# Dense matmuls beside P*V bursts issued as four 32-column tiles, with new orders on all five engines

## The chip, the core and the metric

The kernel runs on one core of one Trainium2 chip. The metric is the time of one execution on the device in microseconds (us). TensorE (PE in the profile; its weight loads are listed as PEld) does the matrix products, VectorE (DVE), ScalarE (ACT) and GpSimd (POOL) the elementwise work, and SyncE (SP) issues most of the transfers (DMAs) between device memory and the core. ScalarE's queue issues the transfers of wk and wv.

## What is computed

A sequence of 2048 tokens of width 512 goes through two branches, and a sigmoid gate for each token mixes the two results. Branch A is an attention with 32 heads of width 16, in four segments of 512 tokens: causal softmax attention inside a segment, and beside it a linear memory that carries the segments before. Branch B is a gated feed-forward layer of width 1792.

```
g = sigmoid((x * gate_w).sum(-1))
for s in range(4):                       # branch A, 512 tokens at a time
    p = softmax(qs @ ks.T * 0.25 + mask);  a_dot = p @ vs
    a_mem = (phi(qs) @ M) / (phi(qs) @ z + 1e-6)
    o = sig(beta) * a_mem + (1 - sig(beta)) * a_dot
    M, z = M + phi(ks).T @ vs, z + phi(ks).sum(0)
a = concat(o) @ wo
b = (gelu(x @ w_gate) * (x @ w_up)) @ w_down
out = g * a + (1 - g) * b
```

## The kernel before

The work is cut into named tasks of a few instructions. For a segment s, `K`, `Q` and `V` are the projections, `G` and `U` the gate and up products of branch B, and `D` the down product together with the product by wo. All of these are dense: 128 rows by 128 weight columns, 512 values long (256 long in `K0`; 384 and 128 long in the last tile of the output). They are made by `mm` (L502) and cut by `pieces` (L506) into tasks of mostly two matmuls, such as `G1_7.0` and `G1_7.2`. Each task name in an order list stands for such a piece.

The attention of a segment has four steps t. A step has four score visits `qkS_tA0`, `B0`, `A1`, `B1`, and in the even steps a fifth, `L`. A score visit is a set of matmuls of 32 rows by 128 columns (L872): four heads at a time, each in its own 32 rows of the array. ScalarE then takes the exponential of all four PSUM banks (L878), GpSimd masks it (L881), and two tasks `pvS_t_j` on TensorE multiply by V (L920, L928). Those are column tiles: 128 rows by 17 weight columns, four heads beside each other at columns 0, 32, 64 and 96. The memory update `mzS` (L839) has the same form with 32 weight columns. So TensorE works in three forms, and passes from one to another at each change of kind: 32-row tiles (scores, and the memory's read `numx` at L792), full 128x128 (dense), and 32-column tiles (P*V and memory update).

PSUM has eight banks. Four belong to the scores and four, `psW0` to `psW3`, go round between all other products.

The order of the work is written out by hand: `ORDER` (L41) has one list of task names for each engine. `schedule` (L238) does not choose an order. It walks the lists, gives PSUM banks to the tasks, and keeps a clock of its own with costs such as `SWITCH` (L32) for a change of form on TensorE and `BLOCK`, `BLOCK_ASK`, `BLOCK_END` (L35) for the fetches of TensorE's instructions. For the first transfers, that clock has fixed times by name, in the table `LANDING` (L37):

```
            if t.name in LANDING:
                avail = max(t.finish + 2.3, LANDING[t.name])
```

Those times do not depend on where a transfer's name stands in its list. The instructions of each engine are then emitted in the order of its list, with semaphore waits for what they read and overwrite.

The start matters for what follows. Eight matmuls on constants, `warm0` to `warm7` (L590), need no data. Then 16 transposes `x0t...` (L599) turn the first segment's x, which arrives in two transfers `x0_0` and `x0_1` into hT (L574, 256 KB each, 1 KB being 1024 bytes). ScalarE and VectorE copy the result to xT, and the 32 pieces of `K0` follow. A piece whose number after the point is 0 or 2 needs the first part of wk (`w_wk0`, 128 KB); the others need `w_wk1` (128 KB) or `w_wk2` (256 KB). Q0 needs `w_wq0` and `w_wq1`, V0 needs `w_wv0` and `w_wv1` (256 KB each), G0 and G1 need `w_wg0` and `w_wg1` (896 KB each). SyncE issues x, wq and wg; ScalarE issues wk and wv.

The names at the end: `D3_3` is the last tile of the output, in two parts of 384 and 128 columns; ScalarE scales and stores the first (L1048) and VectorE the second (L1051).

Of the kernel before, what the change touches and what calls it, by code (L numbers as in the profile page):

```python
# [21 lines left out]
P = 128  # L22
# [12 lines left out]
BLOCK, BLOCK_ASK, BLOCK_END = 254.4, 172, 192  # L35
# [52 lines left out]
    "act": (  # L88
# [14 lines left out]
    "dve": (  # L103
# [37 lines left out]
class Instr:  # L141
    __slots__ = ("fn", "reads", "writes", "est", "dma_sem", "waits", "deps", "inc", "fence")

    def __init__(self, fn, reads=(), writes=(), est=0.1, dma_sem=None):
# [8 lines left out]
        self.waits = []  # L153
        self.deps = []
        self.inc = False
        self.fence = False


class Grp:
# [268 lines left out]
def _build(es, nc, A_x, A_wq, A_wk, A_wv, A_wo, A_beta, B_w_gate, B_w_up, B_w_down, gate_w, out):  # L428
# [33 lines left out]
    gmat = gexp  # L462
# [707 lines left out]
```

## Time and profile before

| | |
|---|---|
| median of 3 runs | 265.47 us (265.13 to 265.95) |
| the profiled execution | 265.32 us |
| its span in the profile | 264.1 us |
| TensorE matmuls, busy | 3153, 261.1 us (99%) |
| ScalarE busy | 209.0 us (79%) |
| VectorE busy | 197.5 us (75%) |
| GpSimd busy | 105.7 us (40%) |
| instruction fetches (DMA queue q8) | 25 packets, 0.41 MB |

The 1.2 us between the span and the execution's time lie around the profiled instructions. A busy TensorE in this profile only means that matmuls are in flight; their ends are modelled and overlap. So it is read by the starts: the difference between the starts of two groups in the timeline is what the first group cost.

### The profile page before, as it was taken

Reading aid. Unit: us, or ns where it says so; the run is one execution under the profiler, and the core shown is the slowest. Engines: PE = TensorE matmul, PEld = TensorE weight load, DVE = VectorE, ACT = ScalarE, POOL = GpSimd, SP = SyncE. Lnnn points to the kernel's source line nnn. Section 1 sums busy time; section 2 is a strip of 40 time slices with the busy share of each in tenths; the row PEclk is TensorE's granted clock in tenths of the full one; section 3 lists DMA queues with packets and bytes.
Section 4 is the critical chain, followed back from the end, with each engine's and each line's share of the span. In section 5 each row is a group of like instructions: output and inputs, shape, how many; then the busy total and the mean of one; then the engine's idle time right before and its main releaser. Section 6 shows DMA issues by size and latency. Waiting matters only on the chain.

```text
span 264.1 us, 7382 instructions
## 1 busy us (share of the span) xinstructions
PE 261.1 (99%) x3153; PEld 117.6 (45%) x3153; DVE 197.5 (75%) x376; ACT 209.0 (79%) x179; POOL 105.7 (40%) x256
## 2 busy tenths in 40 slices
PE   8999999999999999999999999999999999999997
PEld 4644444444444434443544434353444433443453
DVE  0778788999997968889897776779887751485671
ACT  3698988998999788798877887788787787776702
POOL 8206686352600067265300274608470108352510
PEclk9999999999999999999999999999999999999999
DMA  6962117900003894420004251200000021401002
GB/s 224 320 175 49 37 24 196 243 4 0 2 10 112 224 178 81 64 82 0 2 0 67 57 132 32 83 2 20 5 2 0 2 63 31 91 2 42 22 0 82
DMA packets 32769, 18.25 MB, mean 69 GB/s; under 512 B 20576, under 2 KB 32736, under 8 KB 32736
## 3 DMA queue, kind: packets, MB, share of 16 engines
q1 hardware_dynamic: 31632, 16.73, 26.3%
q10 hardware_dynamic: 1104, 1.05, 1.2%
q8 instruction: 25, 0.41, 0.7%
q14 instruction: 8, 0.07, 0.1%
HBM read 9.84 MB, written 2.10 MB: 45 GB/s over the span
## 4 chain that ended last, share of the span: by engine, by line
PE 96%; DMA 1%; ACT 1%; DVE 0%; issue 0%; ACTq 0%
PE psW L503 75%; PE psXALL L872 9%; PE psW L920 6%; PE psXALL L503 3%; PE psW L928 1%; DMA hT<-in_A_x_dram 1%; PE psW L839 1%; ACT pt L878 1%; PE psXALL L792 1%; PE psXALL L599 1%; ACT L878 0%; DVE obf L1051 0%; ACTq L399 0%
## 5 line engine op out<-in xcount | busy, mean ns | idle before, releaser
L878 ACT ACTIVATE pt<-psXALL 128x2048 bf16<-128x2048 f32 x64 | 120.1, 1876 | 27.1 <-PE psXALL L872 23.5
L881 POOL TENSOR_SCALAR_AFFINE_SELECT pt<-pt 128x256 bf16<-128x256 bf16 x128 | 58.8, 471 | 103.0 <-ACT pt L878 98.2
L503 PE MATMUL psW<-xT,wu 128*128 128x512 bf16 x224 | 55.2, 380 | 0.0
L503 PE MATMUL psW<-xT,wg 128*128 128x512 bf16 x224 | 54.2, 380 | 0.0
L503 PE MATMUL psW<-wd,hT 128*128 128x512 bf16 x210 | 54.1, 380 | 0.0
L1019 DVE TENSOR_TENSOR hT<-psW,hT 128x512 bf16<-128x512 f32 x56 | 36.8, 683 | 16.5 <-PE psW L503 16.2
L881 POOL TENSOR_SCALAR_AFFINE_SELECT ptl<-ptl 128x512 bf16<-128x512 bf16 x32 | 22.5, 702 | 38.0 <-ACT ptl L878 36.4
L503 PEld LDWEIGHTS psW<-xT,wu 128*128 128x128 bf16 x224 | 20.3, 98 | 25.7 <-issue 2.7
L503 PEld LDWEIGHTS psW<-xT,wg 128*128 128x128 bf16 x224 | 20.6, 98 | 24.7 <-issue 2.1
L934 DVE STREAM_TRANSPOSE tb<-psW 128x512 f32<-128x512 f32 x32 | 21.5, 699 | 11.7 <-PE psW L928 11.5
L503 PEld LDWEIGHTS psW<-wd,hT 128*128 128x128 bf16 x210 | 19.3, 98 | 23.9 <-issue 3.0
L872 PE MATMUL psXALL<-qT,kpad 32*128 32x320 bf16 (+3 forms) x512 | 25.4, 273 | 0.0
L1003 ACT ACTIVATE hT<-psW 128x512 bf16<-128x512 f32 x28 | 15.7, 596 | 5.5 <-PE psW L503 5.4
L503 PE MATMUL psW<-xT,wk 128*128 128x512 bf16 (+1 forms) x80 | 19.0, 343 | 0.0
L920 PE MATMUL psW<-pt,vaug 128*17 128x192 bf16 (+3 forms) x512 | 18.8, 273 | 0.0
L872 PEld LDWEIGHTS psXALL<-qT,kpad 32*128 32x128 bf16 x512 | 7.6, 92 | 24.5 <-ACT pt L878 15.4
L503 PE MATMUL psW<-wv,xT 128*128 128x512 bf16 x64 | 18.5, 380 | 0.0
L878 ACT ACTIVATE ptl<-psXALL 128x2048 bf16<-128x2048 f32 x8 | 15.0, 1876 | 3.8 <-PE psXALL L872 3.6
L503 PE MATMUL psW<-wo,oT 128*128 128x512 bf16 x60 | 16.8, 380 | 0.0
L1068 DVE TENSOR_SCALAR ost<-psW,omgt 128x512 bf16<-128x512 f32 x9 | 6.7, 746 | 11.9 <-PE psW L503 11.9
L520 DVE CAST hT<-psW 128x512 bf16<-128x512 f32 x19 | 12.8, 684 | 3.7 <-PE psW L503 3.5
L779 POOL COPY exsT<-exs 32x4 f32<-32x4 f32 x64 | 13.9, 217 | 3.7
(104 smaller groups left out, 302.2 us busy)
## 6 DMA issues: line engine op xcount, KB each, us to landing
out_dram<-ost SPq DMA_DIRECT2D x15, 128.0 KB, 1.9
wg<-in_B_w_gate_dram SPq DMA_DIRECT2D x2, 896.0 KB, 7.3
wu<-in_B_w_up_dram SPq DMA_DIRECT2D x2, 896.0 KB, 6.8
wd<-in_B_w_down_dram SPq DMA_DIRECT2D x2, 896.0 KB, 7.2
phkt<-in_A_x_dram SPq DMA_DIRECT2D x3, 512.0 KB, 4.6
vlow<-vaug SPq DMA_DIRECT2D x8, 136.0 KB, 2.8
hT<-in_A_x_dram SPq DMA_DIRECT2D x2, 256.0 KB, 3.9
wq<-in_A_wq_dram SPq DMA_DIRECT2D x2, 256.0 KB, 5.3
```

The costliest lines, as they stand in the source:

```text
L503: return Instr(lambda e: e.matmul(view(), lhsT, rhs, start=first, stop=last), reads=reads, writes=[fkey if fkey is not None else g.key], e ...
L520: alts[DVE] = [Instr(lambda e: e.tensor_copy(dst(), src()), reads=reads, writes=writes, est=dve_t(n))]
L599: task(f"x0t{nm}_{u}", PE, [Instr(lambda e, k=k, a=a, u=u, k0=k0, src=src: e.transpose(src[:, k, a * 128:(a + 1) * 128], xin[:, 2 * u + a, ...
L779: cross = task(f"exsT{s}", POOL, [Instr(lambda e, g=g, c=c: e.tensor_copy(exsT[sl][32 * g:32 * g + 32, c:16:4], exs[32 * c:32 * c + 32, s4 ...
L872: instrs.append(Instr(lambda e, g=g, lhs=lhs, rhs=rhs, c0=c0, ncol=ncol: e.matmul(X[g][:, c0:c0 + ncol], lhs(32 * g), rhs(32 * g), start=T ...
L878: exp_task(s, f"exp{s}_{t}{name}", [Instr(lambda e: e.activation(dst[:], XALL[:, :].rearrange("p (g c) -> p g c", g=4), ACTF.Exp, scale=AT ...
L881: task(f"msk{s}_{t}{name}", POOL, [Instr(lambda e, view=view, pat=pat, base=base: e.affine_select(out=view, in_=view, compare_op=ALU.is_ge ...
L920: instrs.append(Instr(lambda e, t=t, q=q, kb=kb, slot=slot, c0=c0: e.matmul(gp.f32()[32 * q:32 * q + 17, 128 * kb + 64:512], Vaug[sl][:, k ...
L934: task(f"pvt{s}_{t}_{j}", DVE, [Instr(lambda e: e.transpose(Tb[:, j, :], gp.f32()[:, :]), [gp.key], [("Tb", j)], dve_t(512))], grp=gp)
L1003: lambda e, g=g, ft=ft, s=s: e.activation(hT[s % 2][:, ft, :], g.f32()[:, :], ACTF.Gelu_apprx_tanh),
L1019: task(f"Um{s}_{ft}", DVE, [Instr(lambda e, g=g, ft=ft: e.tensor_tensor(hT[sl][:, ft, :], g.f32()[:, :], hT[sl][:, ft, :], ALU.mult), [g.k ...
L1068: DVE: [Instr(lambda e, view=view, gt=gt, tile=tile: e.tensor_scalar(ostage[(4 * s + tile) % N_OST][:], view(), omgt[:, gt:gt + 1], None, ...
```

## The change

A new method `column_runs` looks at TensorE's list. It cuts the list at every task of the 32-row form (`qk` and `numx`). In a stretch between two cuts that holds at least one `pv` or `mz` task, all pieces made only by `mm` are marked. A marked matmul is emitted as four matmuls of 32 weight columns each, at column positions 0, 32, 64 and 96. All four read the same 512 moving values, and write their 32 partitions of the same PSUM bank. Only the last of the four signals.

```
+    def column_runs(tasks):
+        run = []
+        for t in tasks + [None]:
+            if t is not None and t.tiled != "qk":
+                run.append(t)
+                continue
+            if any(u.tiled == "pv" for u in run):
+                for u in run:
+                    if all(i.wide for i in u.alts[PE]):
+                        u.tiled = "pv"
+                        for i in u.alts[PE]:
+                            i.cols = True
+            run = []
...
-                n_ins = 2 * len(t.alts[PE])
+                n_ins = sum(8 if i.cols else 2 for i in t.alts[PE])
...
     def mm(g, view, lhsT, rhs, reads, first, last, n, fkey=None):
-        return Instr(lambda e: e.matmul(view(), lhsT, rhs, start=first, stop=last),
-                     reads=reads, writes=[fkey if fkey is not None else g.key], est=mm_t(n))
+        def f(e):
+            if not ins.cols:
+                return e.matmul(view(), lhsT, rhs, start=first, stop=last)
+            for c in range(0, P, 32):
+                r = e.matmul(view()[c:c + 32, :], lhsT[:, c:c + 32], rhs, start=first, stop=last,
+                             tile_position=(0, c))
+            return r
+        ins = Instr(f, reads=reads, writes=[fkey if fkey is not None else g.key], est=mm_t(n))
+        ins.wide = True
+        return ins
```

`BLOCK_ASK` and `BLOCK_END` go from 172 and 192 to 187 and 207. All five lists of `ORDER` are new; the tasks in them are the same 615 on TensorE. The parts of the lists that the prediction speaks of:

```
 sp, head
-  x0_0 x0_1 w_wq0 w_wq1 w_wg0 x1_0 w_gwb x1_1 w_beta x1_2 x1_3 w_wg1
+  w_wg0 x0_0 x0_1 w_wq1 w_beta x1_1 w_wq0 x1_0 x1_2 w_wg1 w_gwb x1_3
 act, head
-  tload w_wk0 w_wk1 w_wk2 w_wv0 x0ev0b_0 w_wv1 x0ev1_0 K0_1ev
+  w_wk2 w_wk1 w_wv0 w_wk0 tload x0ev0b_0 w_wv1 x0ev1_0 x0ev1_1
 pe, after the eight warm tasks
-  x0t0a_0 x0t0b_0 x0t1_0 K0_0.0 K0_2.0 K0_3.0 x0t0_1 K0_3.1
+  x0t0a_0 x0t1_0 x0t0b_0 K0_3.0 K0_1.0 K0_0.0 K0_2.0 x0t0_1
 pe, one stretch with P*V
-  qk1_0B0 pv0_3_1 pv0_3_0 U1_8.0 U1_11.2 U1_8.2 U1_6.0 qk1_0L
+  qk1_0B0 U1_0.2 pv0_3_1 U1_13.2 U1_9.0 U1_10.0 U1_9.2 pv0_3_0 qk1_0L
 pe, end
-  D3_2.14 D3_2.16 D3_3w0.12 D3_3a0.0 D3_3w1.4 D3_3w1.8 D3_3w1.12 D3_3a1.0
+  D3_2.16 D3_3w0.12 D3_1.16 D3_3a1.0 D3_0.16 D3_3a0.0
```

In the new list of TensorE 22 stretches hold a P*V or memory task. 218 dense matmuls stand in them and become 872.

More of the change, by code (lines that the diff above doesn't have):

```diff
@@ L34 @@
 TABLE = 1.3
-BLOCK, BLOCK_ASK, BLOCK_END = 254.4, 172, 192
+BLOCK, BLOCK_ASK, BLOCK_END = 254.4, 187, 207
 DMA_SPARE = 1.6
@@ L42 @@
     "pe": (
[45 rows of a table removed]
-    "act": (
[14 rows of a table removed]
-    "dve": (
[18 rows of a table removed]
-    "pool": (
[13 rows of a table removed]
[44 rows of a table added]
+    ),
+    "act": (
[15 rows of a table added]
+    ),
+    "dve": (
[17 rows of a table added]
+    ),
+    "pool": (
[7 rows of a table added]
+    ),
[6 rows of a table added]
+    ),
 }
@@ L141 @@
 class Instr:
-    __slots__ = ("fn", "reads", "writes", "est", "dma_sem", "waits", "deps", "inc", "fence")
+    __slots__ = ("fn", "reads", "writes", "est", "dma_sem", "waits", "deps", "inc", "fence", "wide", "cols")
     def __init__(self, fn, reads=(), writes=(), est=0.1, dma_sem=None):
@@ L156, in __init__ @@
         self.fence = False
+        self.wide = self.cols = False
 class Grp:
@@ L236, in add @@
         return task
+    @staticmethod
+    def column_runs(tasks):
[11 more added lines that the diff above has]
+            run = []
     def schedule(self):
@@ L240, in schedule @@
         queue = {e: [named[x] for x in reversed(ORDER[e].split())] for e in ENGINES}
+        self.column_runs([named[x] for x in ORDER[PE].split()])
         n = len(named)
```

177 rows, old and new, of the table ORDER are left out of this document.

## The prediction

> **What bounds the kernel now.** I read the page first, then the waits of TensorE, then its starts in the timeline, and for the head the transfers.
>
> ```profile
> PE 96%; DMA 1%; ACT 1%; DVE 0%; issue 0%; ACTq 0%
> ```
> ```profile
> PE psW L590 <- PEq L1155: 0.8, 1, 0.8
> PE psXALL L599 <- DMA hT<-in_A_x_dram: 0.2, 1, 0.2
> ```
>
> The chain that ended last is TensorE almost all the way, and the waits of TensorE are two: the start of the program, and 0.2 us at 4.36 us, for the first half of x. After that, it always has a matmul ready. So whatever makes its list shorter makes the kernel shorter, and whatever holds it up is lost for good. What the list costs is read from the starts (timeline of TensorE, 38 to 45 us; first column the start, xN the instructions):
>
> ```profile
> 38.26 0.81 PE L839 MATMUL psW<-vaug,phkt 128*32 128x34 bf16 x64
> 39.00 0.60 PE L503 MATMUL psW<-xT,wg 128*128 128x512 bf16 x2
> 39.54 0.40 PE L872 MATMUL psXALL<-qT,kpad 32*128 32x448 bf16 x8
> 39.87 0.60 PE L503 MATMUL psW<-xT,wg 128*128 128x512 bf16 x2
> 40.31 0.59 PE L503 MATMUL psW<-wv,xT 128*128 128x512 bf16 x2
> 40.74 0.59 PE L503 MATMUL psW<-xT,wk 128*128 128x512 bf16 x2
> 43.34 1.03 PE L503 MATMUL psW<-xT,wg 128*128 128x512 bf16 x4
> 44.29 0.62 PE L920 MATMUL psW<-pt,vaug 128*17 128x448 bf16 x16
> 44.73 0.29 PE L928 MATMUL psW<-ptl,vlow 128*17 128x64 bf16 x16
> ```
>
> Two dense matmuls inside a dense stretch take 40.74 - 40.31 = 0.43, 0.216 each. Two with a change of form behind them take 39.54 - 39.00 = 0.54, four take 44.29 - 43.34 = 0.95 instead of 0.86. So a change costs about 0.096. The single starts of the trace give medians of 88 to 97 ns over what the columns need, whichever two forms are changed, and 10 ns more on the second matmul after each entry into the dense form.
>
> **Part 1: fewer changes of form.** Counted along TensorE's list, there are 170 changes before: 64 dense to score, 68 score to dense, 7 score to P*V, 11 P*V to score, 12 dense to P*V, 8 P*V to dense. After, the marked pieces have the form of the P*V bursts: 54, 53, 22 and 21, and none of the last two kinds, 150 in all. 20 x 0.096 = 1.92, and 23 fewer entries into the dense form at 0.010 = 0.23. **-2.15 us**, all on TensorE's path.
>
> **Part 2: a dense matmul as four column tiles.** Not in the trace of before, but its P*V bursts have that form. Sixteen of them, 448 + 320 + 192 + 64 = 1024 columns in each of the four tiles, take 44.73 - 44.29 = 0.44. Two dense matmuls, also 1024 columns, take 0.43. So the four tiles do run side by side, at 0 to 5 ns more for 512 columns; for 218 matmuls that is 0 to +1.1. I take 0: 0.43 and 0.44 differ by a last digit. Weight loads: 64 memory matmuls, each with its own load of 32 columns, take 39.00 - 38.26 = 0.74, less one change 0.64, so 10 ns for load and matmul. A group's four need 40 ns and lie under its 216, also under the 55 ns of the 18 short groups (128 columns) of the last tile. The Trainium skill, "TensorEngine Tiling (Array Packing)", Restrictions and Gotchas, says that column tiling excludes the fast weight load; with the load time of "TensorE: Matmul & The Clock Gate", LDWEIGHTS, (columns over 1.2 per ns) four loads would take 107 ns, and as an estimate the 18 short groups would cost 0.9 us more. The row of 10 ns speaks against it, and the sum goes by the row.
>
> **Part 3: instructions.** 218 x 3 more matmuls and as many loads are 1308 instructions. The page has 6306 of TensorE in 25 fetch packets, 252 each: 5 fetches more. A packet takes 0.7% of 16 engines' span / 25 = 1.2 us. Where marked pieces and bursts stand thickest (the last 15 us) a packet's worth lasts about 5 us by the durations above, so its successor has time to come. Cost 0; if that cover were gone, up to 5 x 1.2 = 6.
>
> **Part 4: the end.** Now the 384-column part is last (`D3_3a0.0`). Its copy on ScalarE takes 0.58, VectorE's of 128 columns took 0.35, and its last matmul is longer: **+0.3**. In the body, the new lists move nine tasks from VectorE to ScalarE, about 0.6 each; at 79% and 75% busy both stay beside TensorE, cost 0.
>
> **Part 5: the head of the transfer queues.** This decides. SyncE's list now begins with `w_wg0`, 896 KB, ahead of x; ScalarE's puts the first part of wk last of four. Issue times on SyncE, and what the transfer page says of two of them (the first x, then wg; last number: us from issue to landing):
>
> ```profile
> 0.81 0.96 SPq L534 DMA_DIRECT2D hT<-in_A_x_dram  x2
> 2.83 0.47 SPq L534 DMA_DIRECT2D wg<-in_B_w_gate_dram  x1
> ```
> ```profile
> hT<-in_A_x_dram SPq DMA_DIRECT2D x1, 256.0 KB, 3.5
> ```
> ```profile
> wg<-in_B_w_gate_dram SPq DMA_DIRECT2D x1, 896.0 KB, 9.1
> ```
>
> x landed at 4.31, wg, issued at 2.83, at 11.9. SyncE's queue (q1) serves in order: in the packet records wg's packets of 1792 bytes begin at 7.4, when the 1024 KB of x and wq ahead of it have gone. How fast bytes move, in two stretches (last number GB/s):
>
> ```profile
> 0.00:4.36 4.36, 3.36 (x9) 1.03 (x9) 0.00 (x0) 1.49 (x2) 3.21 (x14) 1.00 0.48 154
> 4.36:8.20 3.84, 3.84 (x37) 3.42 (x38) 1.14 (x3) 1.25 (x3) 3.67 (x3) 1.00 1.10 358
> ```
>
> 671 KB (of 1000 bytes) by 4.36, then 358 a microsecond, with engines full. Ahead of the end of both `x0_0` and `w_wk0` now stand 896 + 256 KB on SyncE's queue and 768 KB on ScalarE's, 1966 of 1000 bytes. (1966 - 671) / 358 = 3.62: done at 8.0. If the queues take turns by packet (1792 against 1024 bytes for wg, then equal), each gets there at 8.0. Landing follows the last byte by 0.63 (3.68 to 4.31 before). x at 8.6 against 4.31, so the transposes start **4.25 us later**, and K0, 0.8 behind, too. Ends: if SyncE's queue gets ahead (70 of 100 packets), x comes at 7.4, but wk only at 10.05, against K0's start at 5.18: +4.9. The least is wk at 8.4, x earlier: +3.25. Nothing hides it: TensorE has no idle time later to give back.
>
> It is also cold. The timeline from 0.84 us:
>
> ```profile
> 0.84 3.36 PE L590 MATMUL psW<-const-bfloat16-1.0 128*128 128x512 bf16 x8 [0.84 <-PEq L1155]
> 5.18 0.84 PE L503 MATMUL psW<-xT,wk 128*128 128x256 bf16 x3
> 5.82 0.43 PE L599 MATMUL psXALL<-ident,hT 128*128 128x128 bf16 x4
> 6.09 0.60 PE L503 MATMUL psW<-xT,wk 128*128 128x256 bf16 x4
> 6.53 0.39 PE L599 MATMUL psXALL<-ident,hT 128*128 128x128 bf16 x4
> ```
>
> Three 256-column matmuls took 0.64 at 5.18, four took 0.44 at 6.09: half speed until 5.9 (the granted clock reads 1.00 even so; the starts decide), 5.06 us after the first matmul. The warm matmuls now end at about 4.0 and TensorE stands idle for over 4 us. Bounds: full speed at once at 8.6 would save the (5.9 - 4.36)/2 = 0.78 lost before; another 5.06 at half speed loses 2.53. I take the latter, the only warm-up that the trace shows: 2.53 - 0.78 = **+1.75**. By the page "TensorE: Matmul & The Clock Gate", Part 1, the clock is judged in free-running windows of 3.4 us, and a cold stretch would be 3.4 to 6.8 long: as an estimate +0.9 to +2.6.
>
> x's other transfers now stand behind wg's second half, but all bytes of the head had landed by 17.9 before, and the first piece that needs them (`V1_1.2`, 12 us of list after the first transpose) comes after 20.
>
> **Sum.** 265.32 - 2.15 + 0.3 + 4.25 + 1.75 = **269.5 us**. The profiled execution is 0.15 under the median of 265.47, which I leave.
>
> **Rivals.**
> *The head stays as it is* (0.10): the chip serves wg beside x rather than before it, and x lands at 4.3. 265.32 - 2.15 + 0.3 = 263.5, faster. It decides as long as x and wk land before 4.31 + 1.85 = 6.2. Against it: the strict order in q1. Half way, about even at 265.3: 0.02.
> *Late, but at full speed* (0.20): 269.5 - 2.53 = 267.0.
> *Instruction fetch* (0.04): all five extra fetches exposed, 275.5. For it, marked pieces take instructions four times as fast; against, fetches in before come as close as 4.4 us without a hole in the starts.
> *The tiles don't run side by side* (0.02), so the change isn't what it says: 218 x 3 x 0.216 = 141, 406 us. The P*V rows exclude it nearly.
>
> **Numbers.** Forecast 0.62. Low end: 265.32 - 1.85 + 3.25 - 0.4 for a clock mostly open = 266.3; high end: 269.5 + 0.65 for wk at 10.05 + 0.85 for a longer cold stretch + 0.8 for slower column groups = 271.8. Faster by over 0.3% (what can be told from no change) 0.10, same 0.02, slower 0.88.
>
> **What would show it.** Right: TensorE's wait for hT or wk grows from 0.2 to about 4 us; half speed follows; behind it the distance from K0 to the last matmul is some 2 us shorter; marked groups start 216 ns apart. Wrong: the first transpose at 4.4; gaps in the starts inside marked stretches; or waits of TensorE for VectorE or ScalarE, which the new orders would then have made.

## The result, and the profile after

The changed kernel takes 273.12 us (median of 4 runs, 272.82 to 273.43) against 265.33 (265.13 to 265.95) for the kernel before: ratio 1.029, 95% interval 1.0268 to 1.0311. It is slower, as forecast, but 7.8 us slower where 4.2 was said, and above the 271.8 at which the stated range ended. The profiled execution took 272.82 us, its span is 271.5.

The first part of the page, and the chain that ended last, have changed:

```profile
PE 257.3 (95%) x3779; PEld 121.2 (45%) x3807; DVE 195.3 (72%) x367; ACT 215.5 (79%) x191; POOL 104.9 (39%) x256
...
PE 89%; DMA 3%; ACT 2%; POOL 2%; issue 2%; DVE 1%; ACTq 1%; DVEq 0%
```

TensorE's share of the chain fell from 96% to 89%. Part of that fall is only a matter of missing matmul records, which are explained below: of two kernels of the experiments whose head is that of before, `e3`, with 30 records missing, reads 90%, and `e8`, with none missing, 96%. The waits of TensorE in the trace (total, times, longest) say where the rest went:

```profile
PE psXALL L629 <- DMA hT<-in_A_x_dram: 4.3, 1, 4.3
PE psW L527 <- issue: 3.2, 20, 0.2
PE psW L620 <- PEq L1185: 0.8, 1, 0.8
PE psW L527 <- DMA wk<-in_A_wk_dram: 0.8, 1, 0.8
PE psW L950 <- POOL pt L911: 0.5, 1, 0.5
```

The 0.2 us for x have become 4.3, and 0.8 for wk have come. The second line is no loss of time: 3807 weight loads are recorded but only 3779 matmuls, each load has its matmul, and so 28 records are missing. Each of these "waits" is the place of an unrecorded matmul: `e5` below has the same order of the body and all of its 3821 matmuls recorded, and this line is not there. Reading 3.2 us of stall from it would have been an error.

The head in the timeline of TensorE (start, length, group, and what it waited for):

```profile
0.84 3.35 PE L620 MATMUL psW<-const-bfloat16-1.0 128*128 128x512 bf16 x8 [0.84 <-PEq L1185]
8.48 1.04 PE L629 MATMUL psXALL<-ident,hT 128*128 128x128 bf16 x8 [4.28 <-DMA hT<-in_A_x_dram]
10.28 1.01 PE L527 MATMUL psW<-xT,wk 128*128 128x256 bf16 x4 [0.77 <-DMA wk<-in_A_wk_dram]
11.09 0.63 PE L629 MATMUL psXALL<-ident,hT 128*128 128x128 bf16 x4
11.52 0.85 PE L527 MATMUL psW<-xT,wk 128*128 128x256 bf16 x3
12.16 0.63 PE L629 MATMUL psXALL<-ident,hT 128*128 128x128 bf16 x4
...
19.80 0.40 PE L902 MATMUL psXALL<-qT,kpad 32*128 32x448 bf16 x8
```

The last line is the first score visit. Before, it was

```profile
13.45 0.40 PE L872 MATMUL psXALL<-qT,kpad 32*128 32x448 bf16 x8
```

x comes at 8.48 instead of 4.36, and the 256-column matmuls still take 0.21 each (0.64 for three from 11.52), where before four took 0.44 at 6.09. The single starts show half speed until 13.6.

The end, on SyncE's queue:

```profile
266.55 0.33 SPq L564 DMA_DIRECT2D out_dram<-ost  x1
267.11 1.55 SPq L564 DMA_DIRECT2D out_dram<-obf  x1
268.70 0.91 SPq L564 DMA_DIRECT2D out_dram<-ost  x2
269.65 0.45 SPq L564 DMA_DIRECT2D out_dram<-pex  x1
```

Before, the end was the last four matmuls and, after them, the issue of the small store `obf`:

```profile
261.80 0.39 PE L503 MATMUL psXALL<-wo,oT 128*128 128x128 bf16 x4
...
262.60 0.33 SPq L534 DMA_DIRECT2D out_dram<-obf  x1
```

The issue took 0.33 us there. Here it takes 1.55, and three more stores stand behind it.

With those landmarks the whole difference can be laid out (starts in us):

| | before | after | difference | of which new |
|---|---|---|---|---|
| first transpose of x | 4.36 | 8.48 | +4.13 | x late |
| first K0 | 5.18 | 10.28 | +5.10 | +0.97 |
| first score visit | 13.45 | 19.80 | +6.35 | +1.25, half speed |
| last matmul | 261.97 | 267.43 | +5.47 | -0.88, the body |
| end of the span | 264.09 | 271.52 | +7.43 | +1.96, the tail |

And the column tiles themselves, in the timeline of TensorE near the end of the changed kernel:

```profile
265.52 0.50 PE L529 MATMUL psXALL<-wd,hT 128*32 128x384 bf16 x8
265.85 0.60 PE L529 MATMUL psW<-wo,oT 128*32 128x512 bf16 x8
266.28 0.40 PE L529 MATMUL psXALL<-wo,oT 128*32 128x128 bf16 x16
266.50 0.60 PE L529 MATMUL psW<-wo,oT 128*32 128x512 bf16 x8
266.94 0.82 PE L529 MATMUL psXALL<-wo,oT 128*32 128x384 bf16 x16
```

Eight tiles of 512 columns, two full products, take 266.28 - 265.85 = 0.43, exactly what two dense matmuls took before. Four groups of 128 columns take 0.22, 55 ns a group. The last line is four groups of 384 columns, and the last tile of the fourth is the last matmul of the table.

### The profile page after: what moved, and what is told of

Same layout as the page of the kernel before. It is cut to its first block, busy times and chain, and to the rows that moved or that the text cites. A ratio compares the mean times of both kernels' runs of the same rounds, so it can differ in the third digit from the quotient of the medians.

```text
span 271.5 us, 8665 instructions
## 1 busy us (share of the span) xinstructions
PE 257.3 (95%) x3779; PEld 121.2 (45%) x3807; DVE 195.3 (72%) x367; ACT 215.5 (79%) x191; POOL 104.9 (39%) x256
## 4 chain that ended last, share of the span: by engine, by line
PE 89%; DMA 3%; ACT 2%; POOL 2%; issue 2%; DVE 1%; ACTq 1%; DVEq 0%
PE psW L527 54%; PE psW L529 15%; PE psXALL L902 9%; PE psW L950 5%; DMA wk<-in_A_wk_dram 3%; PE psXALL L529 1%; PE psW L958 1%; PE psXALL L527 1%; POOL ptl L911 1%; PE psW L869 1%; PE psXALL L822 1%; ACT ptl L908 1%; ACT pt L908 1%; POOL pt L911 1%; ACTq L564 1%
## 5 line engine op out<-in xcount | busy, mean ns | idle before, releaser
L911 POOL TENSOR_SCALAR_AFFINE_SELECT pt<-pt 128x256 bf16<-128x256 bf16 x128 | 55.5, 445 | 95.5 <-ACT pt L908 90.9
L527 PE MATMUL psW<-xT,wg 128*128 128x512 bf16 x197 | 48.1, 379 | 1.0 <-issue 0.8
L911 POOL TENSOR_SCALAR_AFFINE_SELECT ptl<-ptl 128x512 bf16<-128x512 bf16 x32 | 25.2, 786 | 50.2 <-ACT ptl L908 48.5
L527 PE MATMUL psW<-xT,wu 128*128 128x512 bf16 x162 | 41.0, 380 | 1.0 <-issue 1.0
L527 PE MATMUL psW<-wd,hT 128*128 128x512 bf16 x133 | 34.8, 380 | 0.8 <-issue 0.8
L527 PEld LDWEIGHTS psW<-xT,wu 128*128 128x128 bf16 x168 | 15.2, 98 | 19.7 <-issue 1.9
L527 PEld LDWEIGHTS psW<-wd,hT 128*128 128x128 bf16 x138 | 12.5, 98 | 16.0 <-issue 2.1
L902 PEld LDWEIGHTS psXALL<-qT,kpad 32*128 32x128 bf16 x512 | 7.6, 92 | 24.0 <-ACT pt L908 13.6
L529 PE MATMUL psW<-wd,hT 128*32 128x512 bf16 x288 | 18.2, 380 | 0.0
L950 PEld LDWEIGHTS psW<-pt,vaug 128*17 128x17 bf16 x512 | 12.0, 91 | 10.3 <-POOL pt L911 1.1
L527 PE MATMUL psW<-wv,xT 128*128 128x512 bf16 x55 | 14.8, 379 | 0.1
```

Of the source, the lines that this page charges most:

```text
L527: return e.matmul(view(), lhsT, rhs, start=first, stop=last)
L529: r = e.matmul(view()[c:c + 32, :], lhsT[:, c:c + 32], rhs, start=first, stop=last, tile_position=(0, c))
L902: instrs.append(Instr(lambda e, g=g, lhs=lhs, rhs=rhs, c0=c0, ncol=ncol: e.matmul(X[g][:, c0:c0 + ncol], lhs(32 * g), rhs(32 * g), start=T ...
L911: task(f"msk{s}_{t}{name}", POOL, [Instr(lambda e, view=view, pat=pat, base=base: e.affine_select(out=view, in_=view, compare_op=ALU.is_ge ...
L950: instrs.append(Instr(lambda e, t=t, q=q, kb=kb, slot=slot, c0=c0: e.matmul(gp.f32()[32 * q:32 * q + 17, 128 * kb + 64:512], Vaug[sl][:, k ...
```

## The experiments

My theory after this: the late start (5.1) and its half speed (1.25) come from the order of the first transfers alone; the marking by itself is a gain of about 2 us; and 1.2 us of the tail come from something that the marking moved. The main rival: the new orders of the body cost, and the head is made up for later.

**The head.** Three kernels take the new transfer order out or put it in.

`e1_after_old_head`, the changed kernel:

```
-  sp   w_wg0 x0_0 x0_1 w_wq1 w_beta x1_1 w_wq0 x1_0 x1_2 w_wg1 w_gwb x1_3
+  sp   x0_0 x0_1 w_wq0 w_wq1 w_wg0 x1_0 w_gwb x1_1 w_beta x1_2 x1_3 w_wg1
-  act  w_wk2 w_wk1 w_wv0 w_wk0 tload
+  act  tload w_wk0 w_wk1 w_wk2 w_wv0
```

> The changed kernel with the first transfers of SyncE and ScalarE in the order of before; nothing else changed. Theory (late x and wk cost 5.1 us, the half-speed stretch behind them 1.25 us): the first score visit moves from 19.8 back to about 13.5 us, and 273.1 becomes about 266.8. Rival (the rest of the new orders is what costs, and the late start is made up for later): 270 or more. Rival (the body's new waits come from the shifted head too): 265 or less.

Measured: 265.54 us, 1.0004 of before (0.9982 to 1.0026), and the first score visit at 13.45, to the hundredth where it was. 7.6 us went with the order of twelve and five names. Both rivals fall. The median is 1.3 under what the theory gave. Between the two profiled executions the span is 6.86 shorter: 6.35 in the head, 0.26 in the body and 0.25 in the tail.

`e2_before_new_head` makes the opposite edit in the kernel before.

> The kernel before with the first transfers of SyncE and ScalarE in the new order; nothing else changed. Theory: x lands at about 8.4 and the first part of wk at about 10.2 us, and 265.3 becomes about 271.7 (5.1 us late and 1.25 us at half speed). Rival (part of the loss comes from the new order of TensorE's own first tasks): under 270.

Measured: 272.30 us, 1.0265 (1.0219 to 1.0312); x at 8.1, wk at 9.95, first score visit at 20.14. The kernel before loses as much from the same edit, and the rival falls: from the first score visit to the last matmul (248.51), and from there to the end (2.12), it takes what it took without the edit.

`e6_before_new_sync_head` and `e7_before_new_scalar_head` take one half of that edit each.

> The kernel before with the new first transfers of SyncE alone (wg ahead of x); ScalarE's kept, so wk's first part is first in its queue. Theory (both queues share the transfer engines, and x waits for all of wg): transposes at about 8.3, K0 0.85 behind them, at 9.1 instead of 5.2, and 1.5 us of half speed: 265.2 becomes about 270.7. Rival (wk's place is what costs): 268 or less.

> The kernel before with the new first transfers of ScalarE alone (the first part of wk last of four); SyncE's kept. Theory: x at 4.3, the first part of wk after 768 KB of its queue, at about 8.5 by the rate of before (where the fourth landed at 8.7), K0 at 8.6 instead of 5.2: 3.4 us and up to 1.5 of half speed, 268.6 to 270.1. Rival (wk's part comes early because x and wq are few): under 267.

Measured: 270.25 us (1.0176, 1.0138 to 1.0213) with SyncE's half, 270.92 us (1.0209, 1.0176 to 1.0242) with ScalarE's. Waits of TensorE, first with SyncE's half:

```profile
PE psXALL L599 <- DMA hT<-in_A_x_dram: 3.4, 1, 3.4
```

and with ScalarE's half:

```profile
PE psW L503 <- DMA wk<-in_A_wk_dram: 3.9, 1, 3.9
```

Both rivals fall. Each half alone costs 5 to 6 us, both together 7, because the two waits lie beside each other. That SyncE's half came out near its forecast is partly luck: the transposes started at 7.61, not at 8.3, and the half speed cost 2.15 us instead of 1.5. ScalarE's half cost more than expected: K0 started at 8.92, near the 8.6 foreseen, but half speed lasted to 14.6, so that the first score visit came 6.2 us late, 2.5 of it by the clock.

**The half speed.** `e5_after_warm`, the changed kernel with more warm matmuls:

```
-    for i in range(8):
+    for i in range(22):
         gw = Grp(banks)
```

(with `warm8` to `warm21` in TensorE's list behind `warm7`)

> The changed kernel with 22 instead of 8 warm matmuls, so that TensorE works on constants until about 8 us. x (8.4) and the first part of wk (10.2) land as they did. Theory (the stretch at half speed comes of the idle time before it): K0 starts at 10.3 as it did, but 256-column matmuls take 0.11 instead of 0.21 from there on, which saves 1.7 us: 273.1 becomes about 271.4. Rival (the half speed has another cause, or the wait of 1 to 2 us for wk brings it back): 272.5 or more.

Measured: 270.29 us, 1.0196 (1.0154 to 1.0238). The head in its timeline:

```profile
0.84 7.46 PE L621 MATMUL psW<-const-bfloat16-1.0 128*128 128x512 bf16 x22 [0.84 <-PEq L1186]
8.30 0.62 PE L630 MATMUL psXALL<-ident,hT 128*128 128x128 bf16 x8
10.48 0.60 PE L528 MATMUL psW<-xT,wk 128*128 128x256 bf16 x4 [1.56 <-DMA wk<-in_A_wk_dram]
10.91 0.39 PE L630 MATMUL psXALL<-ident,hT 128*128 128x128 bf16 x4
```

K0 still waits for wk until 10.48, but its matmuls take 0.11 each: 1.6 us of idle time after steady work did not bring the half speed back; 3.4 us (`e6`), 3.9 (`e7`) and 4.3 (the changed kernel) did. From K0 to the first score visit it is 7.95 us, as against 9.52 in the changed kernel: 1.57 saved, where 1.7 was expected. The other 1.1 us came at the tail, as shown below.

Where the trace has records of the clock, the half speed stands in the granted clock itself (third number from the end). A stretch of `e7`, then the half-speed stretch of the changed kernel:

```profile
8.00:14.70 6.70, 5.78 (x31) 4.14 (x32) 1.54 (x5) 0.78 (x2) 0.05 (x1) 0.50 1.06 273
```
```profile
8.50:13.50 5.00, 4.23 (x28) 3.32 (x29) 0.72 (x2) 1.58 (x3) 0.00 (x0) 1.00 1.20 308
```

The trace of the changed kernel has no clock record before 13.62 us, so its 1.00 says nothing there. In `e2`, `e4` and `e7` the record reads 0.50 for 6.83 us, from 7.70, 7.90 and 7.96 on. Counted from TensorE's first work after the wait, half speed lasted 5.2 us in the changed kernel, but 5.9 in `e7`, 6.4 in `e2` and 6.6 in `e4`, which has the changed kernel's own head. So one execution does not tell how long it lasts in the next.

**The marking.** `e3_before_columns`: the kernel before, its orders kept, with `column_runs` and the new `mm`.

> The kernel before, all orders kept, with the marking alone: 221 dense matmuls become 884 column tiles, and changes of form go from 170 to 150. Theory (a change costs 0.096 us, four tiles cost what one full matmul does): 265.3 - 2.1 = 263.2. Rival (more instructions and loads eat the gain): 265 or more.

Measured: 265.14 us, 0.9975 (0.9952 to 0.9999). Much less than the 2.1 us forecast. The last matmul starts 1.31 us earlier (260.65), but the end is only 0.1 earlier: the tail ate it. Of the 1.31, 0.28 is the head, where half speed ended sooner in this execution; the body gained 1.03. The time is the one that the rival gave, but its reason fails: `e11` below has more instructions still and is faster.

`e4_after_no_columns`: the changed kernel without the call.

```
-        self.column_runs([named[x] for x in ORDER[PE].split()])
```

> The changed kernel with no matmul marked, orders kept: changes of form go from 150 to 185. Theory: 35 x 0.096 and 17 more entries into the dense form at 0.010 are 3.5 us, so 273.1 becomes about 276.6. Rival (the stretches have waits that hide the changes, or the column tiles themselves cost): under 275.

Measured: 277.15 us, 1.0444 (1.0409 to 1.0479). From the first score visit to the last matmul 251.7 us against 247.6 with the marking: 4.1 for 35 changes of form. In these orders the marking is worth that, and the rival falls. The issue of `obf` is back at 0.33 us, and the tail 1.2 us shorter. The times differ by 4.0 as well, but not for this alone: the head of `e4` was 0.3 slower, and its profiled execution has 2.2 us outside the span where the others have 1.2. Why it has them stays open.

**The tail.** In the kernel with the marking alone the order of the stores is that of before, and still the last one is slow:

```profile
260.75 0.33 SPq L560 DMA_DIRECT2D out_dram<-pex  x1
261.30 1.38 SPq L560 DMA_DIRECT2D out_dram<-obf  x1
```

In the transfer view of 260.6 to 262.4 us of that kernel stands what the kernel before has not at this place, one packet of q8, an instruction fetch (5.4% of 16 engines over 1.8 us, so 1.56 us long):

```profile
q1 hardware_dynamic: 272, 0.22, 36.8%
q8 instruction: 1, 0.02, 5.4%
```

TensorE has 30 fetches with the marking instead of 25, and the last of them now falls among the stores. The theory: it holds up the issue. If so, moving the fetch by a number of instructions, with nothing done to the stores, must make the long issue come and go. Four kernels do that. `e8_columns_fetch_moved` leaves out the marking of 29 matmuls, `e10_columns_fetch_back` of 16 more, `e11_columns_one_more` adds 22, all three on `e3_before_columns`:

```
 e8   -                for u in run:
      +                for u in run[15:] if len(run) == 24 else run:
 e10  +                for u in [] if len(run) == 24 else run:
 e11  -            if any(u.tiled == "pv" for u in run):
      +            if any(u.tiled == "pv" or u.name in ("V3_1.0", "D2_0.0") for u in run):
```

`e9_after_old_head_fetch_moved` is `e1_after_old_head` with `("U3_3.0", "D2_1.4")` in that line.

> The kernel before with the marking, but 29 matmuls of the long stretch around num2 left unmarked: 174 instructions fewer on TensorE and one change of form more (0.1 us). Theory (with the marking alone the last instruction fetch of TensorE falls together with the last stores, and holds up SyncE's issue of the last one: 1.38 instead of 0.33 us): the last fetch now comes some 5 us before the end or not at all, the last store is issued in 0.33, and 265.1 becomes 264.1 to 264.2. Rival (column tiles at the end delay it in another way): 265.1 to 265.3, with the long issue still there.

> The kernel before with the marking, and now the whole stretch around num2 left unmarked (45 matmuls, not 29): 96 instructions fewer than there, the same number of changes of form. Theory: the last fetch moves back to about 260.6 us, into the last stores, the last issue takes over 1 us again, and 263.9 becomes about 264.9. Rival (fewer tiles are simply better, or no different): 263.9 or less.

> The kernel before with the marking, and two stretches of 12 and 10 dense matmuls without P*V marked as well: 132 instructions more than with the marking alone, no change of form more or less. Theory: the last fetch moves from 260.7 to about 258.2 us, out of the stores, and 265.1 becomes about 263.8. Rival (more instructions cost more): 265.1 or more.

> The changed kernel with the old head, and two stretches of 12 and 10 dense matmuls without P*V marked as well: 132 instructions more, no change of form more or less. Theory (the last fetch at 260.3 us held up the stores): it now comes 2 to 3 us before, the small store is issued in 0.33 instead of 1.30 us, the last matmul starts at 260.8 as before, and 265.5 becomes about 264.4. Rival (the new order of the stores is what makes the end long): 265.3 or more.

| kernel | last fetch packet at | store `obf` issued at | issue lasts | time, ratio to before |
|---|---|---|---|---|
| before | 259.1 | 262.6 | 0.33 | 265.2 |
| e3, marking alone | 260.7 | 261.3 | 1.38 | 265.14, 0.9975 |
| e8, 174 instructions fewer | 258.6 | 261.3 | 0.33 | 263.86, 0.9946 (0.9922 to 0.9970) |
| e10, 96 fewer again | 263.2 | 263.5 | 1.43 | 266.04, 1.0022 (1.0005 to 1.0039) |
| e11, 132 more than e3 | 257.4 | 261.2 | 0.33 | 263.82, 0.9945 (0.9928 to 0.9962) |
| changed kernel | 266.9 | 267.1 | 1.55 | 273.12, 1.029 |
| e5, 28 more | 264.5 | 265.5 | 0.49 | 270.29, 1.0196 |
| e1, old head | 260.3 | 260.5 | 1.30 | 265.54, 1.0004 |
| e9, 132 more than e1 | 258.7 | 261.0 | 0.33 | 264.89, 0.9987 (0.9973 to 1.0002) |

The long issue came in all four kernels whose last fetch starts within 0.6 us before it, and in no other; in `e5`, where the fetch starts 1.0 us before, it is 0.49. In these five the issue ends 0.37 to 0.39 us after the fetch packet does (in the changed kernel the packet takes 266.88 to 268.29, and the issue ends at 268.66). From the start of the last matmul to the end it is 3.3 us in `e3` and `e10` and 2.1 in `e8` and `e11`, and with the new order of the stores 4.1 and 3.8 (changed kernel, `e1`) against 2.9 (`e9`). So the 1.0 to 1.2 us are the fetch's.

The theory was too narrow in one point: the fetch holds up the stores themselves, not the issue alone. `pex`, issued in 0.33 us both times, landed after 3.0 us in `e3` and 1.6 in `e11` (last number):

```profile
out_dram<-pex SPq DMA_DIRECT2D x1, 96.0 KB, 3.0
```
```profile
out_dram<-pex SPq DMA_DIRECT2D x1, 96.0 KB, 1.6
```

The kernel before had a fetch from 259.06 to 260.76 too. A store of 128 KB was issued inside it at 259.59, in 0.33 us, and landed after 2.6 us, the next one after 1.7; but nothing waited for it. Why one store inside a fetch is issued at once and the next must wait is not shown.

That fewer column tiles (`e10`) are slower than more (`e8`) follows from nothing else I know. `e10` came out 1.1 us above its expected time; its profiled execution also waited 1.7 us for wk in the head, and why its median is that high stays open. `e9` came out 0.5 above; its rival falls, and in its profiled execution the head was 0.45 slower. In `e11` the stores read as they did before the change:

```profile
256.88 3.35 SPq L560 DMA_DIRECT2D out_dram<-ost  x3
260.69 0.33 SPq L560 DMA_DIRECT2D out_dram<-pex  x1
261.24 0.33 SPq L560 DMA_DIRECT2D out_dram<-obf  x1
```

e8 and e11 are the fastest versions, 1.3 to 1.4 us under the kernel before.

**Everything as column tiles.** `e12_columns_everywhere`, also on e3:

```
-            if any(u.tiled == "pv" for u in run):
+            if run and run[0].name != "warm0":
```

> The kernel before with every dense matmul behind the first score visit issued as column tiles: some 11,800 instructions instead of 6,306, about 46 fetches, no change of form more or less than with the marking alone. Theory (four tiles cost what one matmul does, and a fetch has 5 us or more): 263.8 to 264.5, up to 1 us more where a fetch meets the stores. Rival (the supply of instructions becomes the limit): 267 or more, with waits of TensorE that nothing releases.

Measured: 265.73 us, 1.0020 (1.0005 to 1.0035). That is 1.2 above the upper end of the theory, though no fetch met the last store (the tail is 2.14). The rival's 267 was not reached, but its mechanism shows once: with 46 fetches, TensorE waited one time for nothing that the profile shows, for 1.2 us, shortly after a fetch packet of 18.20 to 19.35:

```profile
19.21 0.40 PE L525 MATMUL psW<-xT,wg 128*32 128x512 bf16 x4
20.77 0.83 PE L525 MATMUL psW<-xT,wg 128*32 128x512 bf16 x12 [1.16 <-issue]
```

A group of four tiles of 512 columns takes 0.216 us here too (median of 791). The body is 1.9 us longer than that of `e8`; 1.2 of it is this wait, and the rest is not traced to a cause.

## Why the prediction was right in sign and wrong in size

*The head (Part 5): right, with some luck.* x was put at 8.6 and came at 8.44, and the transposes started 4.13 late where 4.25 was said. wk came at 10.15, beyond what an equal share gave (8.6) and next to the other end (10.05). So SyncE's queue did get more than its turn: in the packet records, the last byte of `x0_0` had moved at 7.52, and by then SyncE's queue had moved 1152 KB and ScalarE's 491, which is 70 of 100. x still came near the time that I had worked out for equal shares, because it landed 0.92 us after its last byte and not 0.63; two errors cancelled. K0 started 5.10 late. Half speed lasted 5.16 us after the first transpose, where 5.06 was taken; with 5.9 in `e7`, 6.4 in `e2` and 6.6 in `e4`, the close hit is luck. As an estimate from "TensorE: Matmul & The Clock Gate", Part 1, of the Trainium skill, it is one to two windows, 3.4 to 6.8 us, and these four numbers agree. Because part of the half-speed stretch was spent waiting for wk, it cost 1.25 and not 1.75 in this execution; in `e2` and `e4` it cost 1.8 and 2.0. Together 6.35 against 6.0. The rival "late, but at full speed" was wrong here, and `e5` shows what it would have taken. One sign that I had named failed: from K0 to the last matmul it was to be some 2 us shorter and is 0.37 longer, for the 1.25 of half speed lie behind K0 and the body gave back only 0.88.

*The column tiles (Part 2): right.* 216 ns for four tiles of 512, as for one full matmul. The estimate that I worked out from "TensorEngine Tiling (Array Packing)", Restrictions and Gotchas, of the Trainium skill, 0.9 us for the short groups, does not hold here: they take 55 ns.

*Fewer changes of form (Part 1): the step that failed first.* The -2.15 were put down "all on TensorE's path". The body gained only 0.88; counted in the same way, from the first score visit to the last matmul, it gained 1.14 in `e1`, 1.29 in `e8` and 1.39 in `e11`. The price of a change was right: in `e8` the median of each kind over what its columns need is the same as before within 2 ns. What failed is "all on TensorE's path": waits that the changes had covered came out. In the orders of the changed kernel the single starts show 1.1 us of new holes (counted in `e5`, where no record is missing). The largest, 0.64, is a P*V burst of the first segment that waits for a mask on GpSimd:

```profile
60.56 0.29 PE L958 MATMUL psW<-ptl,vlow 128*17 128x64 bf16 x16
61.33 0.61 PE L950 MATMUL psW<-pt,vaug 128*17 128x448 bf16 x16 [0.48 <-POOL pt L911]
```

`e1` has the same hole with the old head, `e3` has 0.13 there: the new orders made it. I had said that such waits would show, but priced them at 0. With the old orders (`e8`, `e11`) six small holes of 0.06 to 0.15 came in the place of the changes, 0.6 together. Four of them stand in front of a score visit, and there TensorE, now earlier, meets ScalarE not yet done: in `e8` these visits start 0.05 to 0.06 us after an exponential ends. One of the four (ScalarE's exponential, then the visit):

```profile
142.23 1.88 ACT L904 ACTIVATE pt<-psXALL 128x2048 bf16<-128x2048 f32 x1
```
```profile
144.16 0.40 PE L898 MATMUL psXALL<-qT,kpad 32*128 32x320 bf16 x8 [0.15 <-ACT pt L904]
```

*The tail (Parts 3 and 4): the largest miss.* "+0.3" was 1.96. The new order of the last products and stores cost 0.8 (a tail of 2.89 in `e9` and 2.87 in `e4`, which meet no fetch, against 2.12 before), and the last instruction fetch 1.2. Of the 0.8, 0.4 lies before the issue of the last store, which is about the +0.3 of the sum. The other 0.4 lies behind it: the last store is now `pex`, 96 KB, which takes 1.87 us from its issue to the end in `e9`, where `obf`, 32 KB, took 1.49 before. The sum had no term for that. Part 3 asked only whether TensorE would run out of instructions, and answered right for this kernel: its waits show none, and `e12` shows one in 46 fetches. It did not ask what else a fetch packet gets in the way of. The rival of exposed fetches had the right actor and the wrong victim: not TensorE waited, but SyncE and the stores.

The sum of the misses: 0.35 in the head, 1.27 in the body, 1.66 in the tail, 3.3 us, which is all by which the profiled execution (272.82) lies over 269.5.

## What to carry to other kernels

An order that was judged by a model must be read for what the model gives for free. In the clock that the kernel keeps of itself, the first landing times are constants, so moving 896 KB ahead of x, and the first part of wk behind three other transfers, cost nothing there and 7 us on the chip. When a change alters the number of instructions, look at where the fetches fall, not only at whether the engine runs dry: a fetch beside the last stores is on the path. And a gain in the middle of a packed engine is a gain only until the next wait that was just hidden.

## What the runs showed of the hardware that I had not expected

- A full 128x128x512 product as four 32-column tiles costs the same 0.216 us, and 0.055 us at 128 columns; with every dense matmul tiled, 0.216 is still the median (`e12`).
- While an instruction fetch of TensorE (16 KB, 1.17 to 1.56 us in these kernels) was under way, the issue of a small store on SyncE took 1.30 to 1.55 us instead of 0.33, in four of four kernels where they met, and ended 0.37 to 0.39 us after the fetch did. Stores that had been issued landed late as well: after 3.0 us instead of 1.6 (`e3`, `e11`), or 2.6 instead of 1.7 (before). What they share was not tried.
- After steady warm matmuls, 1.6 us of idle time left TensorE at full speed; after 3.4 to 4.3 us without work it ran at half speed, for 5.2 us in the changed kernel. The granted clock reads 0.50 there for 6.83 us in three runs (`e2`, `e4`, `e7`); the changed kernel and `e6` have no clock record at that place, and the 1.00 that a view gives there says nothing.
- Some 28 to 44 matmul records of a trace can be missing. They are not the column tiles' doing: `e5` and `e8` have tiles and miss none, `e2` and `e4` have none marked and miss 38 and 44. The weight loads are complete in all of them, and counting both tells a missing record from a wait.
